# A pair of token blocks multiplied by one Winograd-like scheme: where its operands and raw sums lie, how far ahead they are loaded, and where one weight job and one block's split stand

## The chip, the cores and the metric

The kernel runs on one core of a Trainium2 chip. The metric is the device time of one execution in microseconds (us). A program of this kernel has five engines that work side by side, each in the order written for it: PE (TensorE, matrix products; its weight loads are shown as PEld), DVE (VectorE), ACT (ScalarE), POOL (GpSimd) and SP (SyncE), which issues all DMAs here.

## The reference

Three layers follow one another on an input of 8 batches, 576 positions and 512 channels (8 heads of 64).

```python
rel = pos[:, None] - pos[None, :]
Dmat = np.where(rel >= 0, gamma[:, None, None] ** rel, 0.0)
x = (scale * q @ k.T * Dmat) @ v                 # retention, per head
u = x + (x.transpose(0, 2, 1) @ U @ V).transpose(0, 2, 1)
x = u + np.maximum(u @ w_ch1, 0.0) @ w_ch2       # 512 -> 2048 -> 512
xk = mu_k * x + (1 - mu_k) * x_prev              # x_prev: one position back
xr = mu_r * x + (1 - mu_r) * x_prev
k = np.maximum(xk @ w_k, 0.0)                    # 512 -> 1024
out = 1 / (1 + np.exp(-(xr @ w_r))) * (k * k @ w_v)
```

## The kernel before, in words

The 8 x 576 = 4608 positions form nine token blocks of 512. Every matrix product is done in parts: an operand x is split into a high part h (a cast on ACT to the fp32r type) and a low part l = x - h (a subtraction on DVE), and the product is the sum of wh x uh, wl x uh and wh x ul on PE.

The program has four stretches that matter here.

1. The retention, in 40 steps (8 batches of 5), with hidden products of the first feed-forward layer laid between its instructions. A hidden item (t, f) is the product of block t with one of 16 slices of 128 hidden channels: 12 matmuls with 128x512 outputs into one of two banks h (`hidden_part`, L432), then a relu on ACT into a tile hs (L438) and a store from SP (L443). As there are two banks, an item waits for the hs of the item two before it. Beside this the retention runs "jobs" that stand in a list `waiting`, a stage at each slot. Such a job (`block_weight`) prepares a block of a weight of the last layers: it loads raw words, rebuilds 32-bit numbers from them (ACT L100 and L104, DVE L107), forms sums on POOL (L292 to L295), splits them (ACT L307, POOL L308) and stores the parts (SP L314). There are six of them: keys 0 to 3 and gates 0 and 1. Also in the retention, sums of the weights of the first layer are formed for eight groups and written to memory (`first_sums`); these are the "raw sums" that come back later.
2. The pair. Blocks 5 and 6 are multiplied together by a scheme of seven products instead of eight, in eight groups of 42 matmuls (`first_group`, PE at L1506). The moving operands are seven combinations of the two blocks, named 11, t3, t1, 21, t2, t4 and 22 in the order in which the products use them (`operands`: casts at L747, subtractions into l at L748, differences at L751). The stationary operands are weights or that group's raw sums, split by `split_first` (ACT L361, DVE L362) after `load_first` has fetched them (SP L354, tile fr). The products 1, 7, 5, 2, 6, 4, 3 of a group go to four banks, fa, fc, fd, fb, fa, fc, fd. ACT copies products 1, 7 and 6 out (L1512), DVE adds to these (L1514, L1518, L1522, L1528), ACT applies the relu (L1490), and SP stores (L1492).
3. The tail of the hidden items: blocks 7 and 8, 32 items, sorted so that block 8's items start two slices later. A block is fetched (`fetch_block`, L412, tiles uw) and split in two halves (`split_block`: ACT L419 into uh, DVE L420 into ul). Jobs for the second weight (`second_weight`: load L465, words, sums on POOL) run at its `tick`s.
4. The second feed-forward product, keys, gates and values, from about 490 us to the end.

The order is not left to a scheduler: each engine runs what the program wrote for it in the order of writing. Other work is laid beside the pair by a table, `put(at, fn)`: position 7 * g + i is behind the i-th product of group g. SP is one queue for all loads and stores, in order of writing too, so a store that waits for its tile holds up the loads behind it.

Memory: a pool `big` has 35 tiles ("units") of 4 KB for each partition. During the retention, pools of its own lie beside it. When the retention is over, a second pool `big2` of 16 units is opened over their memory (L1448), and its tiles wait for what lay there. The output xt of the retention's last batch lies in what become units 12 to 14 of `big2`, and is stored from there (L1115, L1116, tile ub in memory).

Before, `operands` puts all of its tiles in `big2`, the difference t included:

```python
gen = operands(x1, 0, whole.pop(PAIR[0]), whole.pop(PAIR[1]), "f", big2)
next(gen)
load_first(0)
load_first(1)
```

The raw sums and their parts are in `big`. Two groups' raw sums are loaded ahead of the pair; group g + 2 is loaded at position 7g + 2 and split at 7(g + 1), behind the first product of the group before its own.

Of the kernel before, what the change touches and what calls it, by code (L numbers as in the profile page):

```python
# [9 lines left out]
F32 = mybir.dt.float32  # L10
F32R = mybir.dt.float32r
# [32 lines left out]
def retention_mixer_kernel(ctx: ExitStack, tc: tile.TileContext, io):  # L44
# [15 lines left out]
    def unit(pool, dt, nm):  # L60
        return pool.tile([128, 2, 512], dt, tag="unit", name=nm)
# [288 lines left out]
    fs, fraw = {}, {}  # L350

    def load_first(g):
        fraw[g] = big.tile([128, 4, 256], F32, tag="unit", name=f"fr{g}")
        nc.sync.dma_start(fraw[g], kept_1[g])  # L354

    def split_first(g):
        x = fraw.pop(g)
        fs[g] = h, l = tuple(
            big.tile([128, 4, 256], F32R, tag="unit", name=f"f{y}{g}") for y in "hl"
        )  # L360
        nc.scalar.copy(h, x)  # L361
        nc.vector.tensor_tensor(l, x, h.bitcast(F32), op=ALU.subtract)  # L362
# [92 lines left out]
    def second_weight(j, pool):  # L455
        raw, got = [], {}
        out = pool if j else big2

        late = j == NF // 2 - 1

        def load():
            for i in range(2):
                r = big2.tile([128, 512], I64, tag="unit", name=f"w2raw{j}_{i}")
                f = j + 8 * i
                nc.sync.dma_start(r, io["moe_w_ch2"][f * 128:(f + 1) * 128, :])  # L465
                raw.append(r)

        def down():
            got["a"] = unit(big if late else big2, F32, f"w2a{j}")
            got["f"] = unit(big if late else big2, F32, f"w2f{j}")  # L470
            for i in range(2):
                high(got["a"][:, i], raw[i])
                low(got["f"][:, i].bitcast(U32), raw[i])

        def fill(i):
            f = got["f"][:, i]
            join(f, got["a"][:, i], f.bitcast(U32))

        def sums():
            x = got["s"] = big2.tile([128, 4, 256], F32, tag="unit", name=f"w2s{j}")  # L480
            f = got["f"]
            a11, a21, a12, a22 = f[:, 0, :256], f[:, 0, 256:], f[:, 1, :256], f[:, 1, 256:]
            s1, s3, s2, s4 = (x[:, i] for i in range(4))
            eng = nc.vector if late else nc.gpsimd
            eng.tensor_tensor(s1, a21, a22, op=ALU.add)
            eng.tensor_tensor(s2, s1, a11, op=ALU.subtract)
            eng.tensor_tensor(s3, a11, a21, op=ALU.subtract)
            eng.tensor_tensor(s4, a12, s2, op=ALU.subtract)

        def part(i, lo, eng):  # L490
            w = (wp, wq)[i]
            if j not in w:
                w[j] = [
                    out.tile([128, 4, 256], F32R, tag="unit", name=f"w2{'pq'[i]}{j}_{x}")
                    for x in range(2)
                ]
            if lo:
                src = got["s"][:, 2 * i:2 * i + 2]
            else:
                src = got["f"][:, :, 256 * i:256 * i + 256]  # L500
            h, l = (x[:, 2 * lo:2 * lo + 2] for x in w[j])
            nc.scalar.copy(h, src)
            eng.tensor_tensor(l, src, h.bitcast(F32), op=ALU.subtract)

        def parts(lo, eng):
            for i in range(2):
                part(i, lo, eng)

        def parts_of_one(i):
            for lo in range(2):  # L510
                part(i, lo, nc.vector)

        return [
            load, *[None] * (5 if late else 1 if j else 2), down, lambda: fill(0), lambda: fill(1), sums,
            *(
                (lambda: parts_of_one(0), lambda: parts_of_one(1)) if late
                else (lambda: parts(0, nc.vector), lambda: parts(1, nc.gpsimd))
            ),
        ]
# [220 lines left out]
                mixing(out[t][i][:, k % 2, :], t, j, k, tp)  # L740
                yield

    def operands(x, q, a, b, nm, where=big):
        def upper(n, src):
            h, l = (unit(where, F32R, f"{nm}{y}{n}_{q}")[:, :, :columns(q)] for y in "hl")
            x[q, n] = h, l
            nc.scalar.copy(h, src)  # L747
            return lambda: nc.vector.tensor_tensor(l, src, h.bitcast(F32), op=ALU.subtract)  # L748

        def less(out, u, v):  # L750
            nc.vector.tensor_tensor(out, u, v, op=ALU.subtract)  # L751

        lower = upper("11", a[0])
        t = unit(where, F32, f"{nm}t_{q}")[:, :, :columns(q)]
        less(t, b[1], b[0])
        yield
        lower()
        lower = upper("t3", t)
        yield
        less(b[0], b[0], a[0])  # L760
        yield
        lower()
        lower = upper("t1", b[0])
        yield
        less(t, b[1], b[0])
        yield
        lower()
        lower = upper("21", a[1])
        two = upper("t2", t)
        yield  # L770
        lower()
        yield
        less(a[1], a[1], t)
        yield
        two()
        lower = upper("t4", a[1])
        yield
        two = upper("22", b[1])
        lower()
        yield  # L780
        two()
        yield
# [23 lines left out]
    def columns(q):  # L806
        return BT if q < NB // 2 else BT // 2
# [7 lines left out]
    with ExitStack() as st:  # L815
# [438 lines left out]
            w.park(big)  # L1254
        jobs = [block_weight(g, big, io["moe2_w_k"], kept_k, "k") for g in range(NG)]
        jobs += [block_weight(g, big, io["moe2_w_r"], kept_r, "r") for g in range(2)]
        jobs = jobs[:NG - 2]
        for at in (1, 3, 5, 7):
            waiting.insert(at, [None])
        for at, job in zip((0, 4), jobs):  # L1260
            waiting.insert(at, job)
        sums = [stage for g in range(HF) for stage in first_sums(g)]

# [189 lines left out]
    x1 = {}  # L1453
    gen = operands(x1, 0, whole.pop(PAIR[0]), whole.pop(PAIR[1]), "f", big2)
    next(gen)
    load_first(0)
    load_first(1)
    for n, (t, f) in enumerate(left):
        for part in range(3):
            hidden_part(t, f, part)  # L1460
# [76 lines left out]

    for g in range(HF - 1):
        put(7 * g, split_first, g + 1)
        if g + 2 < HF:  # L1540
            put(7 * g + 2, load_first, g + 2)
    late_jobs = [block_weight(g, big, io["moe2_w_k"], kept_k, "k", True) for g in (NG - 2, NG - 1)]
    late_jobs += [block_weight(g, big, io["moe2_w_r"], kept_r, "r", True) for g in range(2)]
    for job, ats in zip(late_jobs, (
# [4 lines left out]
    )):  # L1549
        for at, stage in zip(ats, job):  # L1550
            put(at, stage)
    put(30, fetch_block, NB - 2)
    put(40, fetch_block, NB - 1)
    put(45, split_block, NB - 2, 0)
    put(48, split_block, NB - 2, 1)
    put(51, split_block, NB - 1, 0)
    put(53, split_block, NB - 1, 1)
    for at in (46, 49, 52, 55):
        put(at, tick)
    for fn in beside_pair.pop(-1):  # L1560
# [11 lines left out]
    while ready:  # L1572
# [6 lines left out]
        t, f = ready.pop(0)  # L1579
        for part in range(3):  # L1580
            hidden_part(t, f, part)
        tick()
    for n, (q, h, j) in enumerate(ITEMS):
        if n + 4 < len(ITEMS):
# [306 lines left out]
```

## Time and profile before

| | |
|---|---|
| median of 3 runs | 1374.45 us (1373.95 to 1375.54) |
| the profiled execution | 1375.84 us |
| its span in the trace | 1374.0 us |
| PE busy | 1333.8 us (97% of the span) |
| PE weight loads busy | 1092.0 us |
| DVE busy | 932.5 us |
| ACT busy | 673.3 us |
| POOL busy | 341.5 us |

The span runs from the first to the last instruction of the profiled execution; 1.84 us of its time lie outside of it, and its time is 1.39 us above the median of the runs. A row of a timeline gives the start and duration in us, the engine, the line, the operation, output and input by their names in the program (numbers left out), the shape, and, in brackets, how long the engine idled before it and what ended that. A matmul's duration overlaps the next one's, so the pitch of PE's work is read from starts. A busy PE can still be at the lower of its two clocks: then its matmuls take longer.

### The profile page before, as it was taken

The page shows a single profiled execution, that of the slowest core. Times are in us where ns is not written, and L with a number is a line of the kernel's source. Part 1 is how long each engine was busy: PE and PEld are TensorE (multiplying, and loading weights), DVE is VectorE, ACT ScalarE, POOL GpSimd, SP SyncE. Part 2 cuts the span into 40 slices and gives each one's busy share as a digit, 9 for nine tenths or more (in the row PEclk, how much of TensorE's full clock was granted, in tenths as well). Part 3 has the DMA queues.
Part 4 walks back from the last instruction along what each step waited for, and adds up shares of the span by engine and source line. Part 5 has one row for each costly group of instructions (what it writes and reads, how often), then busy time and mean ns, then how long its engine had stood idle before and what let it go on. Part 6 is the DMA issues. An engine that isn't in the chain of part 4 may idle for free.

```text
span 1374.0 us, 25924 instructions
## 1 busy us (share of the span) xinstructions
PE 1333.8 (97%) x10215; PEld 1092.0 (79%) x10215; DVE 932.5 (68%) x1279; ACT 673.3 (49%) x1158; POOL 341.5 (25%) x282
## 2 busy tenths in 40 slices
PE   8999989999899799999999999999999999999998
PEld 5778877887686578787888888888888888888897
DVE  4764376644454422879798898787787787787753
ACT  4653334443466555544443544465465465465431
POOL 1111323221025244122112222203303303303312
PEclk9999999999999899999999999999999999999999
DMA  8967789895479756968878696787076075074272
GB/s 276 344 239 258 238 328 366 290 323 178 162 253 316 259 197 224 311 209 281 291 268 299 229 319 202 276 283 299 1 265 225 6 289 196 31 276 153 90 276 94
DMA packets 128698, 323.66 MB, mean 236 GB/s; under 512 B 14976, under 2 KB 27648, under 8 KB 128576
## 3 DMA queue, kind: packets, MB, share of 16 engines
q1 hardware_dynamic: 128576, 322.01, 66.6%
q8 instruction: 80, 1.31, 0.4%
q14 instruction: 42, 0.34, 0.1%
HBM read 226.54 MB, written 95.42 MB: 234 GB/s over the span
## 4 chain that ended last, share of the span: by engine, by line
PE 61%; DVE 3%; issue 1%; ACT 0%; DVEq 0%; ACTq 0%
PE v L1726 14%; PE h L432 6%; PE gc L604 6%; PE gd L604 6%; PE ga L604 6%; PE kd L1622 4%; PE kc L1622 4%; PE ka L1622 4%; PE gb L604 2%; PE ra L1622 2%; PE kb L1622 2%; PE rc L1622 2%; PE rd L1622 2%; PE c L685 1%; PE c L684 1%; PE c L686 1%
## 5 line engine op out<-in xcount | busy, mean ns | idle before, releaser
L438 ACT ACTIVATE hs<-h 128x512 f32<-128x512 f32 x112 | 66.5, 597 | 146.5 <-PE h L432 139.6
L1682 POOL TENSOR_TENSOR vl<-m,vh 128x512 fp32r<-128x512 f32 (+1 forms) x40 | 47.7, 1193 | 309.1 <-ACT vh L1681 237.5
L563 ACT CAST sbh<-rb 128x1024 fp32r<-128x1024 f32 x64 | 67.4, 1053 | 68.0 <-PE gd L604 51.9
L1726 PE MATMUL v<-vh,wv_0u 128*128 128x512 f32 x288 | 88.7, 389 | 0.0
L1726 PE MATMUL v<-vh,wv_1u 128*128 128x512 f32 x288 | 88.6, 389 | 0.0
L564 DVE TENSOR_TENSOR sbl<-rb,sbh 128x1024 fp32r<-128x1024 f32 x64 | 85.3, 1334 | 3.5 <-ACT sbh L563 3.2
L564 DVE TENSOR_TENSOR sal<-ra,sah 128x1024 fp32r<-128x1024 f32 (+1 forms) x64 | 65.5, 1023 | 27.5 <-PE gd L604 17.5
L563 ACT CAST sah<-ra 128x1024 fp32r<-128x1024 f32 (+1 forms) x64 | 53.6, 837 | 60.1 <-DVE ra L545 17.4
L848 POOL TENSOR_TENSOR kv<-kv,ktab 128x512 f32<-128x512 f32 (+1 forms) x38 | 38.8, 1021 | 177.9 <-DMA kv<-in_kv 143.0
L1682 POOL TENSOR_TENSOR vl<-c,vh 128x512 fp32r<-128x512 f32 (+1 forms) x40 | 62.2, 1574 | 26.2 <-ACT vh L1681 26.2
L1726 PEld LDWEIGHTS v<-vh,wv_1u 128*128 128x128 f32 x288 | 54.1, 188 | 11.2
L1726 PEld LDWEIGHTS v<-vh,wv_0u 128*128 128x128 f32 x288 | 53.9, 188 | 11.0
L1681 ACT CAST vh<-m 128x512 fp32r<-128x512 f32 (+1 forms) x40 | 23.2, 579 | 75.3 <-DVE m L1680 75.3
L1097 DVE TENSOR_TENSOR xt<-mx,xt 128x256 f32<-128x256 f32 (+2 forms) x60 | 28.2, 473 | 43.2 <-PE mx L1093 43.2
L900 DVE TENSOR_TENSOR pm<-up,dtab 128x512 f32<-128x512 f32 (+1 forms) x40 | 25.4, 635 | 46.4 <-PE up L886 43.6
L1726 PE MATMUL v<-vl,wv_0u 128*128 128x512 f32 x144 | 56.0, 389 | 0.0
L1726 PE MATMUL v<-vl,wv_1u 128*128 128x512 f32 x144 | 56.0, 389 | 0.0
L717 ACT ACTIVATE tp<-x2l,omu 128x511 f32<-128x511 f32 x72 | 50.9, 712 | 3.1 <-DMA x2l<-xb 2.4
L648 POOL TENSOR_TENSOR x<-x,ur 128x512 f32<-128x512 f32 x16 | 23.8, 1499 | 109.7 <-DVE x L644 78.3
L621 POOL TENSOR_TENSOR m<-m,ur 128x512 f32<-128x512 f32 x8 | 12.3, 1554 | 136.2 <-ACT m L618 136.2
L1622 PE MATMUL kc<-kht,wk 128*128 128x512 f32 (+1 forms) x160 | 45.5, 368 | 0.0
L1680 DVE SCALAR_TENSOR_TENSOR m<-m 128x512 f32<-128x512 f32 (+1 forms) x40 | 44.4, 1111 | 1.4
(391 smaller groups left out, 3919.5 us busy)
## 6 DMA issues: line engine op xcount, KB each, us to landing
wk<-keys SPq DMA_DIRECT2D x80, 512.0 KB, 6.3
rb<-hp SPq DMA_DIRECT2D x64, 512.0 KB, 6.5
hp<-hs SPq DMA_DIRECT2D x96, 256.0 KB, 3.4
wr<-gates SPq DMA_DIRECT2D x40, 512.0 KB, 6.6
qk<-in_qk SPq DMA_DIRECT2D x32, 512.0 KB, 6.2
kv<-in_kv SPq DMA_DIRECT2D x32, 512.0 KB, 6.8
ra<-hp SPq DMA_DIRECT2D x32, 512.0 KB, 7.3
ur<-ub SPq DMA_DIRECT2D x18, 512.0 KB, 5.5
```

Source lines behind the costliest of these rows:

```text
L432: nc.tensor.matmul(hps[t, f], w.part(lo, k, fo), u[k // 2][:, k % 2, :], start=(part == 0 and k == 0), stop=(part == 2 and k == KD - 1),)
L438: nc.scalar.activation(h, hps.pop((t, f)), AF.Relu)
L563: nc.scalar.copy(hi_, src)
L564: nc.vector.tensor_tensor(lo_, src, hi_.bitcast(F32), op=ALU.subtract)
L604: nc.tensor.matmul(group[g][p], l[:, col(p)], r, start=(h == 0 and j == 0 and i == 0), stop=(i == 2 and last), skip_group_check=True,)
L717: nc.scalar.activation(tp[:, 1:], x[:, :BT - 1], AF.Copy, scale=omu[:, j, k:k + 1])
L848: eng.tensor_tensor(k, k, ktab[:, p, :n].to_broadcast([128, n, NP, D]), op=ALU.mult)
L1097: nc.vector.tensor_tensor(u, ps[:, :n], u, op=ALU.add)
L1622: nc.tensor.matmul(ps[b], l, r[:, i], start=(part == 0 and i == 0 and j == 0), stop=(i == 1 and j == 2), skip_group_check=True,)
L1680: nc.vector.scalar_tensor_tensor(x, x, 0.0, x, op0=ALU.max, op1=ALU.mult)
L1682: eng.tensor_tensor(l, x, h.bitcast(F32), op=ALU.subtract)
L1726: nc.tensor.matmul(vacc[t][o], w.part(lo, g, col(o)), x[:, i, :], start=(g == 0 and i == 0 and j == 0), stop=(g == NG - 1 and i == 1 and j ...
```

## The change

- `operands` takes the second pool only for the parts of t2, t4 and 22. The parts of 11, t3, t1 and 21, and the difference t, come from `big`.
- `load_first` takes `big` for groups 0 to 2 and `big2` from group 3 on; the parts of all raw sums are in `big2`. Three groups are loaded ahead of the pair, and group g + 3 at position 7g + 2.
- The retention does three weight jobs (keys 0 to 2), the pair three (keys 3, gates 0 and 1) at other positions; before, these were two and four.
- A job of the second weight (j) has two idle stages behind its load also for j of 1 and more, where it had one; late ones keep five.
- Blocks 7 and 8 are fetched one position later, block 7's second half is split at 47 instead of 48, and block 8's two halves are split behind the tail's items (7, 0) and (7, 1) instead of at positions 51 and 53 of the pair.

```diff
@@ -350,13 +350,13 @@
     fs, fraw = {}, {}
 
     def load_first(g):
-        fraw[g] = big.tile([128, 4, 256], F32, tag="unit", name=f"fr{g}")
+        fraw[g] = (big if g < 3 else big2).tile([128, 4, 256], F32, tag="unit", name=f"fr{g}")
         nc.sync.dma_start(fraw[g], kept_1[g])
 
     def split_first(g):
         x = fraw.pop(g)
         fs[g] = h, l = tuple(
-            big.tile([128, 4, 256], F32R, tag="unit", name=f"f{y}{g}") for y in "hl"
+            big2.tile([128, 4, 256], F32R, tag="unit", name=f"f{y}{g}") for y in "hl"
         )
         nc.scalar.copy(h, x)
         nc.vector.tensor_tensor(l, x, h.bitcast(F32), op=ALU.subtract)
@@ -511,7 +511,7 @@
                 part(i, lo, nc.vector)
 
         return [
-            load, *[None] * (5 if late else 1 if j else 2), down, lambda: fill(0), lambda: fill(1), sums,
+            load, *[None] * (5 if late else 2), down, lambda: fill(0), lambda: fill(1), sums,
             *(
                 (lambda: parts_of_one(0), lambda: parts_of_one(1)) if late
                 else (lambda: parts(0, nc.vector), lambda: parts(1, nc.gpsimd))
@@ -740,8 +740,9 @@
                 mixing(out[t][i][:, k % 2, :], t, j, k, tp)
                 yield
 
-    def operands(x, q, a, b, nm, where=big):
+    def operands(x, q, a, b, nm, other=big):
         def upper(n, src):
+            where = other if n in ("t2", "t4", "22") else big
             h, l = (unit(where, F32R, f"{nm}{y}{n}_{q}")[:, :, :columns(q)] for y in "hl")
             x[q, n] = h, l
             nc.scalar.copy(h, src)
@@ -751,7 +752,7 @@
             nc.vector.tensor_tensor(out, u, v, op=ALU.subtract)
 
         lower = upper("11", a[0])
-        t = unit(where, F32, f"{nm}t_{q}")[:, :, :columns(q)]
+        t = unit(big, F32, f"{nm}t_{q}")[:, :, :columns(q)]
         less(t, b[1], b[0])
         yield
         lower()
@@ -1254,10 +1255,10 @@
             w.park(big)
         jobs = [block_weight(g, big, io["moe2_w_k"], kept_k, "k") for g in range(NG)]
         jobs += [block_weight(g, big, io["moe2_w_r"], kept_r, "r") for g in range(2)]
-        jobs = jobs[:NG - 2]
+        jobs = jobs[:NG - 1]
         for at in (1, 3, 5, 7):
             waiting.insert(at, [None])
-        for at, job in zip((0, 4), jobs):
+        for at, job in zip((0, 4, len(waiting) + 2), jobs):
             waiting.insert(at, job)
         sums = [stage for g in range(HF) for stage in first_sums(g)]
 
@@ -1453,8 +1454,8 @@
     x1 = {}
     gen = operands(x1, 0, whole.pop(PAIR[0]), whole.pop(PAIR[1]), "f", big2)
     next(gen)
-    load_first(0)
-    load_first(1)
+    for g in range(3):
+        load_first(g)
     for n, (t, f) in enumerate(left):
         for part in range(3):
             hidden_part(t, f, part)
@@ -1537,24 +1538,21 @@
 
     for g in range(HF - 1):
         put(7 * g, split_first, g + 1)
-        if g + 2 < HF:
-            put(7 * g + 2, load_first, g + 2)
-    late_jobs = [block_weight(g, big, io["moe2_w_k"], kept_k, "k", True) for g in (NG - 2, NG - 1)]
+        if g + 3 < HF:
+            put(7 * g + 2, load_first, g + 3)
+    late_jobs = [block_weight(g, big, io["moe2_w_k"], kept_k, "k", True) for g in (NG - 1,)]
     late_jobs += [block_weight(g, big, io["moe2_w_r"], kept_r, "r", True) for g in range(2)]
     for job, ats in zip(late_jobs, (
-        (-1, 5, 6, 8, 9, 10, 11, 12, 13, 15),
-        (8, 16, 17, 18, 19, 20, 22, 23, 24, 25),
-        (19, 26, 27, 29, 30, 31, 32, 33, 34, 36),
-        (30, 37, 38, 39, 40, 41, 43, 44, 45, 46),
+        (-1, 8, 9, 11, 12, 13, 15, 16, 17, 18),
+        (10, 20, 22, 23, 24, 25, 26, 27, 29, 30),
+        (22, 32, 33, 36, 37, 38, 39, 40, 41, 43),
     )):
         for at, stage in zip(ats, job):
             put(at, stage)
-    put(30, fetch_block, NB - 2)
-    put(40, fetch_block, NB - 1)
+    put(31, fetch_block, NB - 2)
+    put(41, fetch_block, NB - 1)
     put(45, split_block, NB - 2, 0)
-    put(48, split_block, NB - 2, 1)
-    put(51, split_block, NB - 1, 0)
-    put(53, split_block, NB - 1, 1)
+    put(47, split_block, NB - 2, 1)
     for at in (46, 49, 52, 55):
         put(at, tick)
     for fn in beside_pair.pop(-1):
@@ -1579,6 +1577,8 @@
         t, f = ready.pop(0)
         for part in range(3):
             hidden_part(t, f, part)
+        if (t, f) in ((NB - 2, 0), (NB - 2, 1)):
+            split_block(NB - 1, f)
         tick()
     for n, (q, h, j) in enumerate(ITEMS):
         if n + 4 < len(ITEMS):
```

PE's order is the same in both. Lines behind 746 are one higher in the changed file.

SP, in the later groups of the pair, around the load of the last group's raw sums (fr from first_106; gates stores are those of a weight job, hp stores those of the pair's results, f_4 being group 4's). Before:

```order
L314 DMA gates_97<-wrh_0_5953 128x512 x2
L314 DMA gates_97<-wrl_0_5954 128x512 x2
L1492 DMA hp_78<-f_4_5979 128x512
L314 DMA gates_97<-wrh_1_5983 128x512 x2
L314 DMA gates_97<-wrl_1_5984 128x512 x2
L1492 DMA hp_78<-f_4_5907 128x512
L354 DMA fr_6027<-first_106 128x1024
L1492 DMA hp_77<-f_5_5999 128x512
```

and now:

```order
L1493 DMA hp_78<-f_3_5902 128x512
L314 DMA gates_97<-wrh_0_5890 128x512 x2
L314 DMA gates_97<-wrl_0_5891 128x512 x2
L1493 DMA hp_78<-f_3_5836 128x512
L354 DMA fr_5950<-first_106 128x1024
L314 DMA gates_97<-wrh_1_5934 128x512 x2
L314 DMA gates_97<-wrl_1_5935 128x512 x2
L1493 DMA hp_77<-f_4_5920 128x512
```

The load stands one group's results earlier (beside f_3 instead of f_4) and ahead of the second pair of gates stores of this job instead of behind it.

ACT, from the last group of the pair to the first tail items (f tiles are the pair's, uh the high parts of blocks 7 and 8, w2a and w2f the second weight's words, hs the tail's results). Before:

```order
L419 CAST uh_0_6216<-uw_0_6064 128x1024
L1490 ACTIVATE f_7_6196<-f_7_6196 128x512
L1512 COPY f_7_6235<-fa_6186 128x512
L419 CAST uh_1_6237<-uw_1_6065 128x1024
L1490 ACTIVATE f_7_6247<-f_7_6247 128x512
L1490 ACTIVATE f_7_6257<-f_7_6257 128x512
L100 ACTIVATE w2a_6261<-w2raw_0_6158 128x512
L104 ACTIVATE w2f_6262<-w2raw_0_6158 128x512
L100 ACTIVATE w2a_6261<-w2raw_1_6160 128x512
L104 ACTIVATE w2f_6262<-w2raw_1_6160 128x512
L1490 ACTIVATE f_7_6204<-f_7_6204 128x512
L438 ACTIVATE hs_0_6283<-h_0_6270 128x512
```

and now:

```order
L1513 COPY f_7_6233<-fa_6188 128x512
L1491 ACTIVATE f_7_6241<-f_7_6241 128x512
L1491 ACTIVATE f_7_6251<-f_7_6251 128x512
L100 ACTIVATE w2a_6255<-w2raw_0_6160 128x512
L104 ACTIVATE w2f_6256<-w2raw_0_6160 128x512
L100 ACTIVATE w2a_6255<-w2raw_1_6162 128x512
L104 ACTIVATE w2f_6256<-w2raw_1_6162 128x512
L1491 ACTIVATE f_7_6206<-f_7_6206 128x512
L438 ACTIVATE hs_0_6277<-h_0_6264 128x512
L419 CAST uh_0_6280<-uw_0_6097 128x1024
L438 ACTIVATE hs_1_6302<-h_1_6289 128x512
L419 CAST uh_1_6305<-uw_1_6098 128x1024
```

Block 8's casts (uh_0_6216 and uh_1_6237 before) stood among the last relus and copies of the pair; now (uh_0_6280 and uh_1_6305) they stand behind the tail's results hs_0 and hs_1.

At the end of the retention the instructions of ACT and DVE for the operands stand in the same order as before; only the tiles' places differ.

## Rows read from the trace of the kernel before

**Rows 1.** Windows: length; PE, PEld, DVE, ACT, POOL busy (count); PEclk, DMA share, GB/s.

```profile
0.00:357.00 357.00, 342.34 (x5772) 272.58 (x5773) 194.84 (x364) 155.29 (x302) 77.88 (x76) 0.99 0.80 280
...
379.00:468.00 89.00, 81.06 (x337) 63.83 (x337) 43.28 (x55) 55.44 (x94) 33.83 (x32) 0.96 0.84 292
...
490.00:1374.00 884.00, 876.75 (x3980) 729.36 (x3978) 673.41 (x839) 440.08 (x729) 226.92 (x170) 1.00 0.61 216
```

**Rows 2.** Waits of PE, 360 to 490 us: total, times, longest, in us.

```profile
PE h L432 <- ACT hs L438: 10.3, 4, 4.2
PE fc L1506 <- ACT f L1512: 4.2, 1, 4.2
PE fa L1506 <- ACT f L1512: 2.5, 4, 1.4
PE fd L1506 <- DVE f L1514: 1.2, 2, 0.8
```

**Rows 3.** Timeline of PE at the end of the retention.

```profile
357.77 1.08 PE L432 MATMUL h<-uh,w_2h 128*128 128x512 f32 x4
...
360.50 1.07 PE L432 MATMUL h<-uh,w_3h 128*128 128x512 f32 x4
...
366.72 1.19 PE L432 MATMUL h<-uh,w_3h 128*128 128x512 f32 x4 [3.35 <-ACT hs L438]
...
371.63 1.70 PE L432 MATMUL h<-uh,w_3h 128*128 128x512 f32 x4 [1.90 <-ACT hs L438]
...
378.82 0.39 PE L1506 MATMUL fa<-fh,w_0h 128*128 128x512 f32 x1
```

**Rows 4.** Timeline of ACT in the same stretch.

```profile
358.46 1.04 ACT L747 CAST fh<-uw 128x1024 fp32r<-128x1024 f32 x1
365.13 1.04 ACT L747 CAST fht<-ft 128x1024 fp32r<-128x1024 f32 x1 [5.63 <-DMA ub<-xt]
...
370.99 0.59 ACT L438 ACTIVATE hs<-h 128x512 f32<-128x512 f32 x1
...
374.52 0.59 ACT L438 ACTIVATE hs<-h 128x512 f32<-128x512 f32 x1
```

**Rows 5.** Timeline of DVE in the same stretch.

```profile
357.51 1.22 DVE L751 TENSOR_TENSOR ft<-uw,uw 128x1024 f32<-128x1024 f32 x1
365.25 1.23 DVE L748 TENSOR_TENSOR fl<-uw,fh 128x1024 fp32r<-128x1024 f32 x1 [6.52 <-DMA ub<-xt]
```

**Rows 6.** Timeline of PE in the pair and the first tail items.

```profile
388.34 0.39 PE L1506 MATMUL fa<-fh,w_0h 128*128 128x512 f32 x1
...
432.20 0.39 PE L1506 MATMUL fd<-fht,fh 128*128 128x512 f32 x1
...
452.42 0.80 PE L1506 MATMUL fc<-fht,w_3h 128*128 128x512 f32 x1 [4.20 <-ACT f L1512]
...
467.96 1.07 PE L432 MATMUL h<-uh,w_0h 128*128 128x512 f32 x4
...
477.71 1.92 PE L432 MATMUL h<-uh,w_0h 128*128 128x512 f32 x4 [4.15 <-ACT hs L438]
...
488.70 1.20 PE L432 MATMUL h<-uh,w_0h 128*128 128x512 f32 x4 [0.95 <-ACT hs L438]
```

**Rows 7.** Timeline of ACT in the pair: the last group's raw sums.

```profile
450.83 1.04 ACT L361 CAST fh<-fr 128x1024 fp32r<-128x1024 f32 x1 [4.33 <-DMA fr<-first]
```

**Rows 8.** Timeline of SP's queue: the load of these sums.

```profile
444.96 0.60 SPq L354 DMA_DIRECT2D fr<-first  x1
```

**Rows 9.** Timeline of ACT around the pair's end.

```profile
470.23 1.05 ACT L419 CAST uh<-uw 128x1024 fp32r<-128x1024 f32 x1
...
474.36 0.64 ACT L100 ACTIVATE w2a<-w2raw 128x512 f32<-128x512 f32 x1
...
477.07 1.07 ACT L438 ACTIVATE hs<-h 128x512 f32<-128x512 f32 x2
```

**Rows 10.** Timeline of DVE in the pair: a subtraction beside POOL's work.

```profile
436.06 2.28 DVE L362 TENSOR_TENSOR fl<-fr,fh 128x1024 fp32r<-128x1024 f32 x1 [3.85 <-POOL wrl L308]
```

## The prediction

> **What bounds the kernel now.** I read the windows first [rows 1]. In the long last stretch PE is busy 876.75 of 884 us at full clock: what happens there is PE's own work, the change doesn't touch it, and whatever the stages ahead gain or lose is passed on whole. In the retention PE is busy 342 of 357 us. The changed stretch lies between, and there PE has 81.06 busy us of 89. The waits of PE say what it waited for [rows 2]: nine waits on ACT's copies of products (hs, f) and two on DVE's sums, none on a DMA directly. So the bound is PE, held up in three places, and I sized each by PE's timeline against a floor. The floor of the pair stage is its group pitch: 388.34 - 378.82 = 9.52 us for 42 matmuls [rows 3, 6], 0.2267 each; a hidden item of 12 matmuls is 2.72.
>
> A: end of the retention. From the item at 360.50 four items remain to the pair's first matmul: 360.50 + 4 x 2.72 = 371.38. It starts at 378.82 [rows 3]: 7.44 lost.
> B: the pair. 467.96 - 378.82 = 89.14 against 8 x 9.52 = 76.16: 12.98 lost, 4.20 of it in one wait [rows 6].
> C: the first tail items. 488.70 - 467.96 = 20.74 for five items that need 13.60: 7.14 lost.
> Together 27.6, which no edit here can exceed by much, as every matmul stays in its place.
>
> **A, first operands in the old pool.** PE's waits there are on hs, and hs stands on ACT behind the casts of the pair's operands. ACT idles 5.63 before the cast at 365.13 and DVE 6.52 before the subtraction at 365.25, both released by the DMA that stores xt, the retention's last output [rows 4, 5]: their tiles lie in the second pool over that output. DVE had finished ft at 357.51 + 1.22 = 358.73, and the cast that its subtraction needs ends at 358.46 + 1.04 = 359.50 [rows 4, 5]. With the tiles in the old pool the chain starts at 359.46 (the next instruction here starts just before the modelled end of the one it waits for) and not 365.25: 5.79 earlier. The two waits: hs at 370.99 moves to 365.20 and ends at 365.79, before its item is due (360.50 + 2 x 2.72 = 365.94), so that wait goes; so does the 3.35 of the item before, whose hs stood behind the first cast. What is late next is the hs at 374.52: it comes to 368.73, its item can start at 369.4 and is due at 368.66: 0.7 is left. Without pauses of 3.35 and 1.90 the slow stretch goes as well: from 371.63 to 378.82 two items took 7.19, not 5.44 [rows 3], with 1.70 where a quadruple takes 1.07, which is the lower of the two clocks. A = 7.44 - 0.7 = 6.7; bounds 5.8 (the start alone moves) and 7.4.
>
> **B, raw sums two groups ahead.** The 4.20 us wait is on ACT's copy of a product that stands behind a cast of raw sums (fh<-fr), which idled 4.33 until its load had landed, at 450.83 [rows 6, 7]. The load was issued at 444.96 on SP [rows 8], 5.9 before. In the program it stands beside the third product of group 5, which begins at 432.20 [rows 6]: SP reached it 12.8 us late, behind weight and result stores that wait for their writers. So issue lag and landing take 18.6. The lead is five of a group's seven products, 6.8 us, before, and twelve, 16.3, after; and the fourth weight's loads and stores (3 MB in all) leave this queue, with the lag with them. SP's rows above show it ahead of the last job's second gates stores, no longer behind them. I expect the load of the last group some 8 us ahead of its cast. After the wait the remaining 54 matmuls took 467.96 - 452.42 = 15.54 and not 12.24, so about 2.5 of lower clock goes with it; 4.2 + 2.4 = 6.6.
>
> The rest of B, 6.4, is the waits of fa on ACT (2.5 in 4) and of fd on DVE (1.2 in 2) [rows 2], the slower first matmuls after each, and stalls too short for the list. They arise where a job's step stands ahead of a copy. The removed job takes from ACT eight instructions (0.64 for a weight word [rows 9]) and the moved block two casts of 1.04, 7.2 of 55.44 busy us [rows 1]; from DVE go two joins and two subtractions of 1.23, from POOL eight of 32 instructions. Following the new order by hand with these durations, every group runs without a wait but the last, whose fifth product waits 0.6 to 1.0 for ACT's copy of the first, behind block 7's two casts. One size there depends on neighbours: the subtraction at 436.06 took 2.28 beside a POOL instruction, and such a one 1.23 elsewhere [rows 5, 10]; I take the worse, 1.0. B = 12.98 - 1.0 = 12.0. Bounds: 6.6 (only the long wait goes) and 13.0.
>
> The Trainium skill (SBUF — State Buffer, Who interferes with whom) says that a two-input DVE instruction and a reading POOL instruction lock each other out of a shared port. The row of 2.28 agrees in kind. By the rule strictly applied group 7's subtraction meets no POOL work after the move and the residue would be 0.6 instead of 1.0.
>
> **C, block 8's split to the tail.** The third tail item starts at 477.71 after 4.15 of waiting [rows 6], on the hs at 477.07, which ends ACT's queue: relus, a cast uh at 470.23, four weight words from 474.36, relus [rows 9]. That cast and the one before it (2 x 1.04 on ACT) and their two subtractions (2 x 1.23 on DVE, ahead of the sums that the relus need) go behind the first hs. Then the chain counted from the pair's end is: DVE's last sum of a product to 0.7, its relu to 1.3, four words of 0.64 or, overlapped, 0.55 to 3.5 to 3.9, a relu and hs to 4.7 to 5.1. The item is due at 2 x 2.72 = 5.44, so the wait goes, and with it the lower clock behind it (a quadruple of 1.92 at 477.71, 1.07 at 467.96 [rows 6]). The moved casts stand behind hs 0 and 1; block 8's first item needs the last of their results some 1.4 us after it is there. Part of the 0.95 at 488.70 stays: C = 6.6. Bounds 0 (the wait reappears behind the moved casts) and 7.1.
>
> **The fourth weight in the retention.** It adds there 8 ACT, 2 DVE and 8 POOL instructions, two loads and eight stores. ACT is busy 155, DVE 195 and POOL 78 of 357 us [rows 1]. They stand behind instructions that wait for something else, at nothing; with that cover gone ACT's four words would cost up to 4 x 0.64 = 2.6, most of which PE's next hidden item would hide. I keep 0, and 2.6 as the bound. The extra idle step of the second weight moves tail work one item later and nothing else: 0.
>
> **Sum.** 6.7 + 12.0 + 6.6 = 25.3; span 1374.0 - 25.3 = 1348.7. The profiled run's time lies 1.84 above its span and 1.39 above the median, so 1348.7 + 1.84 - 1.39 = 1349.2, say 1349.
>
> **Rivals.**
> 1. The long waits go, the short ones stay or move (for: ten instructions change place near the copies; against: ACT and DVE both have less to do). B = 6.6: 1349.2 + 5.4 = 1354.6.
> 2. The change doesn't do what it says at the retention's end: the first operands wait for other holders in the old pool, which now also carries the fourth weight until its stores are out. For: SP stays in the hs stores for 5 us there; against: the tiles next in turn are long read. A = 0: 1355.9.
> 3. The tail's wait is only moved: hs 0 is in time by 0.3 us alone. C = 0: 1355.8.
> 4. Slower: raw sums become late in several groups. They now share sixteen slots with the late operands, and a load behind a slot that is free late blocks SP for all stores behind it. It decides where issue lag and landing (18.6 in the one case seen) pass the new lead of 16.3. In groups 2 to 6 each would cost 4.2 + 2.4 = 6.6, together 33: the pair takes 76.2 + 33 = 109, 20 more than now, less A and C: 1374.45 + 20 - 6.7 - 6.6 = 1381. Against: the lag has to stay although the queue carries less.
>
> **How the numbers follow.** Forecast 0.60; rival 1 0.20, 2 0.08, 3 0.04, 4 0.05; 0.03 for gains that other delays eat up. 0.2%, some 2.7 us, is what a measurement of this kernel can tell from no change. The forecast and rivals 1 to 3 are all faster: 0.92; 0.03 the same, 0.05 slower. The upper bounds of A, B and C are 7.4 + 13.0 + 7.1 = 27.5: 1347.0, and 1346 with the spread of the runs; at the top the range takes in rivals 1 to 3 and the retention's 2.6: 1355.9 + 2.6, some 1359. The forecast's own range is 1346.5 to 1353.
>
> **What would show it.** A: no DMA ahead of the second operand's cast, pair start near 372. B: no wait on a raw sum's DMA at ACT, pair 76 to 78 us long. C: no wait over 1 us on hs after the pair, hs 0 ahead of the moved casts. All three clocks then stay at the upper level between 357 and 490. The forecast fails if PE shows waits on fh or fl (late raw sums), if the retention's stretch to 357 grows by over 2, or if the stretch behind 490 shrinks or grows.

## The result, and the profile after

The changed kernel takes 1351.8 us (median of four runs, 1351.02 to 1356.5) against 1374.85 (1373.95 to 1375.54): a ratio of 0.984 with a 95% interval of 0.9817 to 0.9863. The forecast was 1349 us, with a range of 1346 to 1359. Run again later beside other kernels it took 1352.12 against 1374.27, a ratio of 0.9842 (0.9827 to 0.9857). The profiled execution takes 1351.9 us with a span of 1350.1: 23.9 less than the span before.

The waits of PE from 350 to 475 us in the kernel after (totals, times, longest); here [rows 2] had four lines with eleven waits:

```profile
PE fa L1507 <- ACT f L1513: 1.6, 1, 1.6
PE h L432 <- ACT hs L438: 0.5, 1, 0.5
```

The windows of the same kernel answer to [rows 1] (length; PE, PEld, DVE, ACT, POOL busy with counts; granted clock, DMA share, GB/s):

```profile
0.00:357.00 357.00, 340.01 (x5765) 270.25 (x5766) 194.04 (x365) 159.86 (x310) 85.59 (x84) 0.98 0.82 287
357.00:372.00 15.00, 14.49 (x64) 11.46 (x64) 12.83 (x14) 9.29 (x12) 0.00 (x0) 1.00 0.85 278
372.00:450.00 78.00, 76.41 (x337) 62.96 (x336) 42.89 (x54) 51.65 (x87) 26.27 (x24) 1.00 0.85 293
450.00:468.00 18.00, 18.00 (x81) 14.88 (x81) 8.25 (x11) 13.63 (x25) 2.94 (x5) 1.00 0.59 207
468.00:1350.00 882.00, 875.69 (x3974) 728.11 (x3972) 666.53 (x836) 439.34 (x727) 225.39 (x170) 1.00 0.62 216
```

From 357 us on the granted clock is 1.00 in every stretch: the three drops to the lower level, one in each of [rows 1]'s 379 to 468 us (0.96) and the two stretches beside it, are gone with the waits ahead of them. The kernel before, in these two:

```profile
357.00:379.00 22.00, 16.76 (x65) 13.04 (x65) 14.55 (x14) 10.63 (x13) 0.00 (x0) 0.92 0.47 162
...
468.00:490.00 22.00, 16.89 (x67) 13.18 (x66) 6.41 (x10) 11.83 (x21) 2.83 (x4) 0.92 0.48 168
```

The retention holds 8 more instructions of ACT and of POOL, and by 357 PE has done 2.3 busy us less.

PE's timeline answers to [rows 3, 6]:

```profile
361.93 1.07 PE L432 MATMUL h<-uh,w_3h 128*128 128x512 f32 x4
...
370.94 1.20 PE L432 MATMUL h<-uh,w_3h 128*128 128x512 f32 x4 [0.51 <-ACT hs L438]
...
373.80 0.39 PE L1507 MATMUL fa<-fh,w_0h 128*128 128x512 f32 x1
...
447.63 0.50 PE L1507 MATMUL fa<-fht,fh 128*128 128x512 f32 x1 [1.59 <-ACT f L1513]
...
451.85 1.07 PE L432 MATMUL h<-uh,w_0h 128*128 128x512 f32 x4
...
457.29 1.07 PE L432 MATMUL h<-uh,w_0h 128*128 128x512 f32 x4
...
465.45 1.07 PE L432 MATMUL h<-uh,w_0h 128*128 128x512 f32 x4
```

With the floors of the prediction (10.88 us from the item at 361.93 to the pair, 76.16 for the pair, 13.60 for five tail items) each stage's loss is read off:

| | lost before | lost after | gain | forecast gain |
|---|---|---|---|---|
| A, retention's end | 7.44 | 373.80 - 361.93 - 10.88 = 0.99 | 6.45 | 6.7 |
| B, pair | 12.98 | 451.85 - 373.80 - 76.16 = 1.89 | 11.09 | 12.0 |
| C, first tail items | 7.14 | 465.45 - 451.85 - 13.60 = 0.00 | 7.14 | 6.6 |
| retention up to the last stretch of items | start 360.50 | start 361.93 | -1.43 | 0 |
| behind the tail's sixth item | 885.30 | 884.65 | 0.65 | 0 |
| span | 1374.0 | 1350.1 | 23.9 | 25.3 |

At the retention's end ACT no longer idles for the store of xt [rows 4, 5]; the second operand's cast follows the first:

```profile
359.90 1.04 ACT L748 CAST fh<-uw 128x1024 fp32r<-128x1024 f32 x1
360.83 1.05 ACT L748 CAST fht<-ft 128x1024 fp32r<-128x1024 f32 x1
362.13 0.60 ACT L438 ACTIVATE hs<-h 128x512 f32<-128x512 f32 x1 [0.25 <-PE h L432]
```

### The profile page after: what moved, and what is told of

Its sections match the earlier page's. It is cut to its first block, busy times and chain, and to the rows that moved or that the text cites. A ratio compares the mean times of both kernels' runs of the same rounds, so it can differ in the third digit from the quotient of the medians.

```text
span 1350.1 us, 25914 instructions
## 1 busy us (share of the span) xinstructions
PE 1324.6 (98%) x10215; PEld 1087.7 (81%) x10215; DVE 924.5 (68%) x1279; ACT 673.8 (50%) x1158; POOL 340.2 (25%) x282
## 4 chain that ended last, share of the span: by engine, by line
PE 90%; DVE 4%; DMA 3%; issue 2%; ACT 1%; POOL 0%; SPq 0%; DVEq 0%; POOLq 0%; ACTq 0%
PE h L432 21%; PE v L1726 14%; PE ga L604 6%; PE gc L604 6%; PE gd L604 6%; PE ka L1622 4%; PE kd L1622 4%; PE kc L1622 4%; PE gb L604 3%; PE ra L1622 2%; PE kb L1622 2%; PE rd L1622 2%; PE rc L1622 2%; PE fa L1507 2%; PE fd L1507 2%
```

## Experiments

Each kernel's stages were read from its own profile as in the table above. "Stretch" is a part of the retention, from the 26th to the last copy of xn on ACT (L1038 before, L1039 after); it was 227.95 to 342.45, 114.50 us, before, and 226.79 to 344.44, 117.65, after.

| kernel | A lost | B lost | C lost | stretch | median us | ratio (95%) |
|---|---|---|---|---|---|---|
| u_block8 | 1.01 | 1.91 | 5.79 | 117.74 | 1358.49 | 0.9891 (0.9869-0.9912) |
| u_ahead | 0.92 | 6.35 | 0.00 | 117.76 | 1355.28 | 0.986 (0.9837-0.9883) |
| u_weight | 0.99 | 11.30 | 0.00 | 114.79 | 1360.23 | 0.9905 (0.9883-0.9927) |
| u_pool | 6.75 | 1.88 | 0.00 | 119.45 | 1360.04 | 0.9897 (0.9877-0.9918) |
| u_weight_late | 0.99 | 5.90 | 0.77 | 116.31 | 1354.68 | 0.9854 (0.9834-0.9874) |
| s_pool_ahead | 0.99 | 8.34 | 6.63 | 114.69 | 1362.09 | 0.9906 (0.9883-0.9929) |
| s_weight | 7.44 | 3.38 | 7.24 | 119.51 | 1367.78 | 0.9942 (0.9921-0.9962) |
| v_split | 0.99 | 0.00 | 0.47 | 117.77 | 1350.48 | 0.9826 (0.9799-0.9853) |
| v_late | 0.98 | 0.01 | 0.44 | 115.52 | 1349.52 | 0.9824 (0.9808-0.984) |
| v_late1 | 0.99 | 0.00 | 0.44 | 116.04 | 1348.17 | 0.9812 (0.9797-0.9827) |
| after_again | 0.99 | 1.89 | 0.00 | 118.01 | 1352.12 | 0.9842 (0.9827-0.9857) |

A run's time strays by some us (1370.26 to 1378.76 for the kernel before, on the chip of the first four experiments), most of it early in the retention (the 26th copy of xn starts between 222.62 and 228.21 in these profiles); a stage's loss repeats to 0.1 us. So the stages are what the verdicts rest on. Ratios are to the kernel before on the same chip.

**u_block8** undoes the move of block 8's split.

```diff
+    put(51, split_block, NB - 1, 0)
+    put(53, split_block, NB - 1, 1)
...
-        if (t, f) in ((NB - 2, 0), (NB - 2, 1)):
-            split_block(NB - 1, f)
```

> The changed kernel with block 8's two splits put back at positions 51 and 53 of the pair. Theory (the casts' and subtractions' place ahead of the tail's first result makes the tail wait): hs 0 of the tail now ends some 0.6 us before its item is due; two casts (2.1 us) on ACT and two subtractions (2.5) on DVE ahead of it bring it 2.5 to 4.5 us late, the lower clock follows: 4 to 7 us more, 1356 to 1359. Rival (the lighter pair leaves room, so the place no longer matters): 0 to 1.5 us more, 1352 to 1353.

The pair's loss stays, and the tail's wait is back, 3.91 us against 4.15 before. On ACT, in this kernel, the relus again wait behind the casts, and hs is late. The first relu's row names no releaser; it starts as DVE's sum, itself behind the second subtraction, ends (ACT, then DVE):

```profile
452.78 1.05 ACT L419 CAST uh<-uw 128x1024 fp32r<-128x1024 f32 x1
455.77 1.23 ACT L1491 ACTIVATE f<-f 128x512 f32<-128x512 f32 x2 [1.94 <-issue]
...
459.62 1.07 ACT L438 ACTIVATE hs<-h 128x512 f32<-128x512 f32 x2
```
```profile
453.86 1.23 DVE L420 TENSOR_TENSOR ul<-uw,uh 128x1024 fp32r<-128x1024 f32 x1 [2.12 <-ACT uh L419]
455.00 0.68 DVE L1523 TENSOR_TENSOR f<-fc,f 128x512 f32<-128x512 f32 x1
```

C is this move's: 5.8 of 7.1 come back with it, and nothing with the pools, the lead or the job (0.00 each in u_pool, u_ahead and u_weight). The later fetches of blocks 7 and 8 and the idle stage of the second weight were not undone singly.

**u_pool** puts all operands and t back in the second pool, all raw sums and their parts in the old one.

```diff
-            where = other if n in ("t2", "t4", "22") else big
+            where = other
...
-        t = unit(big, F32, f"{nm}t_{q}")[:, :, :columns(q)]
+        t = unit(other, F32, f"{nm}t_{q}")[:, :, :columns(q)]
```

> The changed kernel with all the pair's operands and the difference t back in the second pool and all raw sums and their parts in the old one. Theory (the first operands wait for the store of the retention's last output): the stretch from the last retention items to the pair is 6 to 7 us longer, the pair and the tail as now: 1358 to 1360. Rival (other holders of the units, or the raw sums' places, matter as well): under 3 us or over 10 us more.

A is 6.75 again, B and C stay at 1.88 and 0; the median lies at the upper end of what the theory said. The two moves, of the operands and of the raw sums, were not undone apart. The cast of the second operand idles for the store as in [rows 4]:

```profile
368.55 1.04 ACT L748 CAST fht<-ft 128x1024 fp32r<-128x1024 f32 x1 [5.72 <-DMA ub<-xt]
```

**u_ahead** shortens the raw sums' lead to what it was.

```diff
-    for g in range(3):
+    for g in range(2):
         load_first(g)
...
-        if g + 3 < HF:
-            put(7 * g + 2, load_first, g + 3)
+        if g + 2 < HF:
+            put(7 * g + 2, load_first, g + 2)
```

> The changed kernel with two raw sums up front and group g+2's load at 7g+2, as before; pools, jobs and splits stay changed. Theory (the lead sets the raw sums' wait): the loads of groups 3 to 7 are issued 0 to 5.6 us behind their place in the program and land some 6 us later, so a lead of 6.8 us leaves two to four groups 2 to 5 us late, with the lower clock after the longer ones: 8 to 20 us more, 1360 to 1372. Rival (the fourth weight's transfers made the lag, and they are gone): 0 to 2 us more, 1352 to 1354.

The pair loses 4.5 us more: neither. Three casts of raw sums wait for their load, 2.12, 0.31 and 1.01 us; PE's longest wait is 2.21. It is not on a raw sum's product but on the last group's fifth, behind block 7's casts, where the changed kernel waits 1.59. Read from the first matmul of a group to that of the next, less 9.52, the last three groups lose 0.77, 1.46 and 4.12; in the changed kernel they lose 0, 0 and 1.89. The last of the three casts, on ACT:

```profile
433.57 1.05 ACT L361 CAST fh<-fr 128x1024 fp32r<-128x1024 f32 x1 [1.01 <-DMA fr<-first]
```

**u_weight** puts the fourth job back in the pair, at its old positions, and leaves the lead.

```diff
-        jobs = jobs[:NG - 1]
+        jobs = jobs[:NG - 2]
...
+        (30, 37, 38, 39, 40, 41, 43, 44, 45, 46),
```

> The changed kernel with the fourth weight job back in the pair at the old positions; pools, lead and block 8's split stay changed. Theory (a lead of 16.3 us covers most of the lag of 18.6 seen before): the long wait stays away or is 2 us, short waits on ACT's copies come back, 1 to 4 us more in the pair, up to 1.4 less in the retention: 1350.5 to 1355. Rival (the job's steps made the pair's waits): 6 to 11 us more, 1358 to 1363.

The theory fell, and the time is the rival's. No cast of raw sums waits, yet the pair loses 11.3: 0.75, 2.35, 0.22, 1.53 and 6.46 in its last five groups. PE waits 4.66 in the last one for ACT's copy of its first product. ACT stood behind a relu, this behind DVE's sum at 450.83, and that behind block 7's two subtractions. DVE's timeline in this kernel:

```profile
445.31 2.14 DVE L420 TENSOR_TENSOR ul<-uw,uh 128x1024 fp32r<-128x1024 f32 x1 [2.74 <-POOL wrl L308]
447.38 0.68 DVE L1523 TENSOR_TENSOR f<-fc,f 128x512 f32<-128x512 f32 x1
449.69 1.23 DVE L420 TENSOR_TENSOR ul<-uw,uh 128x1024 fp32r<-128x1024 f32 x1 [1.63 <-ACT uh L419]
```

The row puts the 2.74 us down to POOL. What ended last is ACT's cast of the same half, which the subtraction reads; it stands behind two casts of the job (ACT, then POOL):

```profile
443.15 1.12 ACT L307 CAST wrh<-wrcf 128x512 fp32r<-128x512 f32 x2
444.18 1.04 ACT L419 CAST uh<-uw 128x1024 fp32r<-128x1024 f32 x1
```
```profile
439.89 3.24 POOL L308 TENSOR_TENSOR wrl<-wrf,wrh 128x512 fp32r<-128x512 f32 x2 [0.69 <-ACT wrh L307]
443.83 2.54 POOL L308 TENSOR_TENSOR wrl<-wrcf,wrh 128x512 fp32r<-128x512 f32 x2 [0.70 <-ACT wrh L307]
```

The cast ends at 445.22, and the subtraction starts 1.13 us after the cast's start, as in the changed kernel (cast 440.03, subtraction 441.15), where POOL has been idle since 438.30. A wait for POOL's reads of a unit is not shown. What the job adds to this chain is its two casts ahead of the cast (444.18 - 443.15 = 1.03) and a subtraction of 2.14 beside POOL's work instead of 1.22 (0.92).

**u_weight_late** is u_weight with block 7's halves split at 48 and 50, not 45 and 47, to tell the place of the split from the job's own steps.

> The changed kernel with the fourth weight job back in the pair, and block 7's halves split at positions 48 and 50 instead of 45 and 47. Theory (with the job in the pair, the subtraction of block 7's first half waits for POOL, the last reader of the unit it writes, and pushes the copy of the last group's first product): three positions later POOL is done, the wait of 4.66 us and the lower clock behind it go, the pair's loss falls from 11.3 to 4 to 5.5, the run to 1352 to 1356. Rival (the job's steps themselves fill ACT and DVE): the loss stays at 9 or more, 1357 or more.

B falls from 11.30 to 5.90, a little above the theory's 4 to 5.5, and the run's time is in its range. The place of the split made 5.4 of it, all in the last group (6.46 to 1.05), though not through the wait on POOL that the theory named. Both halves moved, and which of them brings how much isn't shown; v_split below shows that without the job the second half's place alone costs 1.89. What stays are short waits on copies and sums (0.2 to 1.3 us each) which come with the job's steps: the four groups ahead lose 0.77, 2.33, 0.22 and 1.52, as in u_weight.

**s_pool_ahead** is the kernel before with the pools and the lead alone changed.

> The kernel before with the places of operands and raw sums and the lead of the raw sums changed, and nothing else. Theory (three separate losses): the retention's end loses 1.0 instead of 7.4, no cast waits for a raw sum, the pair loses 6 to 7 instead of 13, the tail 7 as before: 1360 to 1364. Rival (in the pair the fourth job and the splits set the time, and another wait takes the raw sum's place): the pair loses 10 to 13: 1365 to 1369.

A loses 0.99, C 6.63, the median lies in the theory's range; the pair loses 8.34, less than the rival's 10 and more than the theory's 7. Its longest wait, 2.75, is again on a copy, behind block 7's casts and subtractions, which stand behind the job's last casts as in u_weight: part of what the lead gives is taken by the next wait.

**s_weight** is the kernel before with the fourth job moved, the other three at their new positions, and nothing else.

> The kernel before with the fourth weight job moved into the retention and the other three at their new positions in the pair, and nothing else. Theory (the job's stores make SP late, so its move alone shortens the last raw sum's wait): the pair loses 6 to 8 instead of 13, retention's end and tail stay: 1367 to 1369. Rival (only the lead takes that wait away): the pair loses 11 or more: 1372 to 1375.

The pair loses 3.38, less than either theory said; the median is in the theory's range only because the retention's stretch grew by 5.0 us as well. The load of the last raw sums is issued 4.5 us earlier than in [rows 8], although this pair began 3.0 later, and their cast idles for nothing that the list shows (SP's queue and ACT, in this kernel):

```profile
440.43 0.39 SPq L354 DMA_DIRECT2D fr<-first  x1
```
```profile
445.91 1.05 ACT L361 CAST fh<-fr 128x1024 fp32r<-128x1024 f32 x1
```

**v_split** is the changed kernel with block 7's second half split at position 50, to remove the 1.59 us wait that is left.

```diff
-    put(47, split_block, NB - 2, 1)
+    put(50, split_block, NB - 2, 1)
```

> The changed kernel with the second half of block 7 split behind the last group's second product (position 50) instead of behind the sixth of the group before (47). Theory (the last wait of the pair, 1.59 us, is on a copy that stands behind this cast and its subtraction): the wait goes, the pair loses 0 to 0.3 instead of 1.9: 1349.5 to 1350.5 beside 1351.8. Rival (the cast then pushes the third product's sum or the tail's first relus): 0 to 2 us more than the changed kernel.

The wait's chain in the changed kernel, on DVE and on ACT, is the subtraction, a sum that ends at 446.44, a relu and the copy:

```profile
444.62 1.23 DVE L420 TENSOR_TENSOR ul<-uw,uh 128x1024 fp32r<-128x1024 f32 x1 [1.64 <-ACT uh L419]
```
```profile
446.48 0.63 ACT L1491 ACTIVATE f<-f 128x512 f32<-128x512 f32 x1 [1.89 <-DVE f L1523]
447.01 0.57 ACT L1513 COPY f<-fa 128x512 f32<-128x512 f32 x1
```

With the split at 50 the pair takes 76.16: no loss. 0.47 comes back in the tail. The median is 1.3 below the changed kernel's, inside what the runs stray.

**v_late and v_late1** were made for the retention's stretch, which the table shows 3 us longer in every kernel that loads the job's words there as the changed one does (117.65 to 118.01; 119.45 and 119.51 in two in which a drop of the clock falls into it) than with the job in the pair (114.50 to 114.79, and 116.31 in u_weight_late). Both are v_split with the job's load later.

```diff
         jobs = jobs[:NG - 1]
+        jobs[2] = [None, None, jobs[2][0], *jobs[2][3:]]     # v_late
+        jobs[2] = [None, jobs[2][0], *jobs[2][2:]]           # v_late1
```

> The changed kernel with block 7's second half split at position 50, and the third weight job of the retention loading its words two slots later, behind the loads of step 3 and ahead of those of step 4 of the last batch; its words are rebuilt where they were. Theory (the job's load, issued into DMA engines already full, makes PE stand 1.6 to 2.2 us in the middle of the low-rank matmuls near 310 us, with nothing in the program to wait for): the pause there goes or falls under 0.5, the stretch from the 26th to the last copy of xn (117.7 us with the job in the retention, 114.7 without) falls to 115 to 116.5: 1347 to 1349. Rival (the job's own steps lengthen that stretch, wherever its load stands): it stays at 117 or more, 1349.5 to 1351; or the words come late and ACT holds the stage up: 118 or more.

> The same with the load one slot later only, directly behind the loads of step 3. Theory: these loads land as early as without the job, but the DMA engines stay full past 310, so the pause stays at 1 us or more and the stretch takes 116.5 to 117.7: 1348.5 to 1350.5. Rival (the pause comes from step 3's loads being late, not from full DMA engines): the pause goes as in the kernel with two slots.

> The changed kernel as it is, beside these on the same chip: 1350 to 1353, the stretch 117.7, the pause 1.6 to 1.9, the pair's loss 1.9.

In the changed kernel PE stands still between the fifth and the sixth of eight matmuls that wait for nothing in the program:

```profile
309.73 0.41 PE L1058 MATMUL g<-xs,ust 64*32 64x128 f32 x5
311.77 0.41 PE L1058 MATMUL g<-xs,ust 64*32 64x128 f32 x3 [1.63 <-issue]
```

With the load two slots later the eight run through, as before the change. PE's row in v_late:

```profile
310.34 0.42 PE L1058 MATMUL g<-xs,ust 64*32 64x128 f32 x8
```

The theory holds for v_late's stretch (pause gone, 115.52), while its median, 1349.52, lies above the 1347 to 1349 that was expected and is not clear of v_split's. It failed for v_late1: the pause is 0.17 and the stretch 116.04, although the DMA engines' share from 308 to 312 is 1.06. So a full share at the moment of the pause is not enough to cause it. What does go with the pause is the instruction queue, whose 16 KB packets stand in the trace (times in us):

| kernel | packet near 308: start, end | matmul 6 of 8 starts | pause | end of packet to matmul |
|---|---|---|---|---|
| after | 309.4, 310.5 | 311.77 | 1.63 | 1.2 |
| after_again | 309.2, 310.3 | 311.58 | 2.09 | 1.3 |
| v_split | 307.0, 308.0 | 309.44 | 1.93 | 1.4 |
| u_weight_late | 307.5, 308.4 | 309.71 | 1.00 | 1.3 |
| v_late1 | 307.0, 307.9 | 309.35 | 0.17 | 1.5 |
| before | 307.5, 308.6 | no pause | 0 | |
| v_late | 308.0, 309.0 | no pause | 0 | |

PE resumes 1.2 to 1.5 us after such a packet in all five, at the same instruction, and so it does in the four other kernels that pause (u_ahead and u_block8 1.82, u_pool 2.09, s_weight 2.21). In the four that don't, the packet had ended 1.35 to 1.9 us before that matmul was due. The packets stand under one queue for the whole core, and whose instructions this one brings is not seen. The Trainium skill (Runtime: NRT & Kernel Launch, Instruction fetch mechanics) says that an engine's instructions are fetched through a DMA queue of its own in blocks of 16 KiB, and that the cost at a block's edge is mostly hidden. The packets' size agrees; if the packet is PE's, up to 2.2 us is not hidden here. That the job's loads, issued from 300.56 to 302.46, delay the fetch is what moving them points to. They can't be all of it: u_weight_late has no such load and pauses 1.00. How the packets queue behind each other is not seen in these runs and stays open.

v_late1 at 1348.17 beats both kernels: 1374.27 and 1352.12 on the same chip. after_again came out as expected but for its stretch, 118.01, and its pause, 2.09.

## Why the prediction was right

The time was 2.8 us above the forecast, the direction and range held, and no rival took its place.

- **A** was right in mechanism and size: 6.45 for 6.7. What was named as late next, the hs behind the operand's cast, is the 0.51 us wait at 370.94. u_pool, which undoes the places alone, gives 5.8 of it back.
- **B** was right in its sum, 11.1 for 12.0, and wrong in how it was split. "4.2 + 2.4 = 6.6" was given to the raw sums' long wait, for the lead and the shorter queue together, and 6.4 to the steps of the job and of block 8. The runs show no such parts. The job's move alone takes B from 12.98 to 3.38 (s_weight); the lead and the pools alone take it to 8.34 (s_pool_ahead): 9.6 and 4.6, more than the 11.1 of both. In the changed kernel undoing the lead costs 4.5, undoing the move 9.4. The two overlap, since either ends the long wait: one makes SP's queue shorter, the other starts earlier. In u_ahead, u_weight and s_pool_ahead the last group loses most (4.12, 6.46 and 3.07), at a wait behind block 7's split, whose place none of the three edits touches.
- The last wait of the pair was placed rightly (the fifth product behind block 7's casts) and priced at 1.0 where it took 1.59 and the stage lost 1.89: the relu ahead of the copy waited for DVE's sum behind the subtraction at 444.62. That subtraction took 1.23, not the 2.28 of [rows 10], as POOL was idle then; so the worse of the two sizes was taken and the wait was still longer. Which step of the order followed by hand came out too short is not on record; in the trace the chain runs from that subtraction through DVE's sum and the relu. v_split, which moves that cast and subtraction alone, removes all of it.
- **C** was right: 7.14 for 6.6, the moved casts cost nothing behind the first results, and u_block8 gives 5.8 of it back.
- **The fourth weight in the retention** was mis-sized: "I keep 0, and 2.6 as the bound" stands against 3 us in the stretch. The bound was worked out for ACT's words. Its load was never priced: "They stand behind instructions that wait for something else, at nothing" speaks of the engines' instructions alone. v_late gets 2.2 us of the stretch back by the load's place alone (117.77 in v_split to 115.52); the 0.7 to 1.0 us above the kernels with the job in the pair stays unexplained. In the one profile of after an earlier part of the retention ran 1.2 us faster than in that of before, which hides some of it in the sum.
- Rival 1 (short waits persist) is what u_weight_late shows with the job in the pair, 4.8 us in the four groups ahead of the last; with the job gone they go. Rival 4 did not come: the last group's load is issued at 420.24 and its cast stands at 434.45, 14 us later, and waits for nothing.

## What to carry to other kernels

Price a stage by its own floor and list every wait in it, but do not give two edits a share each of one wait that either of them would end: undo them singly. When work is moved into a stretch with idle engines, price its DMA as well as its instructions, and look at where the load falls. A unit of a rotating pool carries the wait for its last reader with it: the store of xt held ACT up for 5.63 us [rows 4] through the unit alone. Where a row names a releaser, look at when the instruction's other inputs were ready: the 2.74 us put down to POOL in u_weight ended with ACT's cast.

## What the runs showed of the hardware that was not expected

- PE can stand 1.0 to 2.2 us in the middle of a run of matmuls with nothing that the profile shows to wait for, always at the same instruction; in the changed kernel with block 7's second half split at 50 (1.93), two loads of 512 KB issued one slot later reduced it to 0.17, two slots later to nothing.
- The lower of PE's two clocks (1.2 against 2.4 GHz) does not follow from the length of one wait: after the wait of 2.21 us in u_ahead (446.36) PE ran at it, with matmuls of 0.63 us where they take 0.39 to 0.40 at the upper one, and after that of 2.75 us in s_pool_ahead (453.10) the clock stayed up. In the pair of the changed kernel, where the longest wait is 1.59, the clock stayed up.
- A subtraction on DVE that started while POOL was at work took 2.14 us (u_weight, 445.31) against 1.23 four us later. It ended 1.08 us after POOL's instruction (447.45 and 443.83 + 2.54 = 446.37). So did that of [rows 10], at 436.06 + 2.28 = 438.34, 1.08 after the end of POOL's row there, 437.26:

```profile
434.68 2.58 POOL L308 TENSOR_TENSOR wrl<-wrcf,wrh 128x512 fp32r<-128x512 f32 x2
```

  The Trainium skill (SBUF — State Buffer, Who interferes with whom) says two-input DVE work and POOL's reads exclude each other; these rows agree. Here it was DVE that waited, until POOL's instruction, begun earlier, was done: two of POOL's subtractions took 2.54 us with DVE idle as well (u_ahead, 430.28).
